# Top-k attention into a Sinkhorn mixture of experts, one core: low parts of the last group's weights and sums of stored outputs through accumulating DMAs, gates copied in a later turn

## The chip, the cores and the metric

The kernel runs on one core of a Trainium2 chip. A core has TensorE (PE in the profile; its weight loads are shown apart as PEld), VectorE (DVE), ScalarE (ACT), GpSimd (POOL) and SyncE (SP), each with a queue of its own that it works through in order, and 16 DMA engines that all queues share. SP issues nearly all DMAs of this kernel. The metric is the time of one execution on the device in microseconds, lower is better.

## The reference

```python
# attention: 4 batches, 8 heads, 576 positions, 64 wide
scores = (1/8) * q @ k.T
scores = where(scores >= the 32nd largest of the row, scores, -1e9)
attn   = softmax(scores);  out = attn @ v
x = out as [N=2304, D=512]
# mixture of experts, 8 experts, hidden width F=1024
P = exp(x @ w_gate - max)
8 times: P /= row sums + 1e-9;  P /= column sums + 1e-9;  P *= N / E
out = sum over e of P[:, e:e+1] * (relu(x @ w1[e]) @ w2[e])
```

The row and column scaling of P (Sinkhorn) is done on all 2304 rows at once, so no gate is known before the last row of attention is.

## The kernel before

The products are done in fp32r with every operand split into a high part (the value rounded to fp32r) and a low part (value minus high part); each product of the reference is three matmuls: high x high, high x low, low x high. A split is one ScalarE copy (`hi_act`, L83) and one subtraction, on GpSimd (`lo_pool`, L86) or VectorE (`lo_dve`, L89).

**Turns.** The 2304 rows are 18 pieces of 128 rows, 9 blocks of 256. Five blocks (`BOARD`) go through the experts in turns: a turn takes one expert for the blocks that are on board, two at a time in most turns. In a turn the expert's weights are loaded by SP (`wr`), split (`wh` on ScalarE, `wl` on GpSimd), the hidden layer is made (L469), stored as `hh` and `hl`, and the second layer is made (L584). The outputs of a turn aren't gated yet: ScalarE copies them to a tile `y` (L592) and SP stores them in DRAM (`spill`). `y` is a ring of four buffers (`YB`) that several steps share, among them `gates`. Turns 16 to 19 have two blocks on board, turns 20 to 23 one.

**Attention** runs beside the turns, at a higher priority: scores on TensorE (L122, L123), top-k on VectorE (L138, L141), exponentials on ScalarE, a transposition by DMA, and the weighing of the values on TensorE (L269). Its last stage belongs to turn 12. It ends with the gate logits (L387) and `sinkhorn`, whose eight rounds have one small matmul each (L444). Then `stages_until` calls `gates`, which transposes the gates of the last four blocks on TensorE (L715, into tile `pc`), copies them to two `y` tiles (L718) and stores them in DRAM, and `right_factors`, which makes the last group's right operands.

**Stored outputs.** `stored` takes the ungated outputs back, piece by piece: SP loads one to a `y` tile (L606), ScalarE multiplies it by its gate (L607), VectorE adds it to `acc` (L609); after eight experts SP writes the piece to the output. There are 80 such steps. `some` does two of them after a hidden tile of turns 20 to 23 (`feeding`), and two for each hidden call of the last group.

**The last group.** The other four blocks (`LAST`, 1024 rows) are done at the end, expert by expert, with Strassen's scheme in the Winograd form: seven products in place of eight. There are 64 calls, 32 of `hidden_pair` and 32 of `outputs_pair`. Each begins with `left_factors`: SP loads 512 KB of weights to a tile `wr` (named `wf` in rows, L682), GpSimd makes four sums `st` of its quarters (L690; also named `wf`), and both are split: `rh` and `rl` from `wr`, `sh` and `sl` from `st`. `wr` and `st` take turns in a ring of three buffers; `rh`, `rl`, `sh` and `sl` have two buffers each. Then come 42 matmuls (L708). `hidden_pair` gates its results (L747), and `all_factors` makes the right operands of the next products: differences on VectorE (L774), splits by L83 and L89.

The order in which instructions stand on each engine is made when the program is built, by a scheduler that goes by priorities and a model of the timeline; `tc.issue_after` ties an instruction behind another.

Of the kernel before, what the change touches and what calls it, by code (L numbers as in the profile page):

```python
# [44 lines left out]

PARKED = 4
ALONE, LATER = range(0, 4), range(4, 8)
WR, WB, XR, NS, RAW, YB, HF = 3, 6, 3, 3, 3, 4, 5


@with_exitstack
def kernel(
# [366 lines left out]
    def sinkhorn():  # L419
# [17 lines left out]
        for i in range(8):  # L437
# [8 lines left out]
            nc.vector.reciprocal(cr, cp)  # L446
            nc.vector.tensor_tensor(P if i == 7 else Q, Q, cr[:, None, :].to_broadcast([128, NT, E]), op=OP.mult)

    def convert(src, shape):
        wr = wp.tile(shape, F32, name="wr", bufs=WR)  # L450
        nc.sync.dma_start(wr, src)
        return split_weights(wr, shape)

    def split_weights(wr, shape):
# [6 lines left out]
    def products(ps, f0, seat, n, wh, wl, k0):  # L461
        nk = wh.shape[1]
        cs = slice(seat.c0, seat.c0 + n)
        for fo in range(512 // n):
            fs = slice((f0 + fo) * 128, (f0 + fo + 1) * 128)
            i = 0
            for kk in range(nk):
                for a, x in ((wh, seat.xh), (wh, seat.xl), (wl, seat.xh)):
                    nc.tensor.matmul(ps[:, fo, :], a[:, kk, fs], x[:, k0 + kk, cs],  # L469
                                     start=(i == 0), stop=(i == 3 * nk - 1))  # L470
                    i += 1

    def hidden(seat, n, s, wh, wl):
        m = 512 // n
        for f0 in range(0, 2, m):
            ps = ps1.tile([128, m, n], F32, name="p1")
            products(ps, f0, seat, n, wh, wl, 0)
            with tc.high_priority(offset=2 * BIG):
                done = store_hidden(seat, slice(2 * s + f0, 2 * s + f0 + m), slice(seat.c0, seat.c0 + n), ps)
            if feeding:  # L480
                some(done, 2)

# [53 lines left out]
            store_hidden(seat, ft, slice(0, 256), ps)  # L536

    def store_hidden(seat, ft, cs, src):
        nc.scalar.activation(seat.hh[:, ft, cs], src, AF.Relu)  # L539
        return nc.vector.scalar_tensor_tensor(seat.hl[:, ft, cs], src, 0.0, seat.hh[:, ft, cs].bitcast(F32),  # L540
                                              op0=OP.max, op1=OP.subtract)

    ready = {}

# [51 lines left out]
    def stored():  # L596
        for blk in BOARD:
            for piece in BLOCKS[blk]:
                t = tile_id[piece]
                acc = accp.tile([128, 512], F32, name="acc", bufs=2)  # L600
                for e in range(E):
                    g = P[:, t, e:e + 1]
                    y = acc if e == 0 else op_.tile([128, 512], F32, name="y", bufs=YB)
                    while (t, e) not in spill:
                        yield False
                    nc.sync.dma_start(y, spill[t, e])  # L606
                    nc.scalar.activation(y, y, AF.Copy, scale=g)  # L607
                    if e:
                        nc.vector.tensor_tensor(acc, acc, y, op=OP.add)  # L609
                    if e == E - 1:  # L610
                        store_rows(nc.sync, acc, piece)
                    yield True

    more = stored()

    def some(ins, n):
        with tc.issue_after(ins.ins):
            for _ in range(n):
                if not next(more, False):
                    break  # L620
# [55 lines left out]
        return f  # L676

    def left_factors(*src):
        wr = wf.tile([128, KD, 256], F32, name="wf", bufs=3)
        rows = KD // len(src)  # L680
        for i, w in enumerate(src):
            nc.sync.dma_start(wr[:, i * rows:(i + 1) * rows], w)  # L682
        a11, a21 = wr[:, 0:2, 0:128], wr[:, 0:2, 128:256]
        a12, a22 = wr[:, 2:4, 0:128], wr[:, 2:4, 128:256]
        st = wf.tile([128, 4, 2, 128], F32, name="wf", bufs=3)
        for i, (a, b, op) in enumerate((
            (a21, a22, OP.add), (st[:, 0], a11, OP.subtract),
            (a11, a21, OP.subtract), (a12, st[:, 1], OP.subtract),
        )):
            nc.gpsimd.tensor_tensor(st[:, i], a, b, op=op)  # L690
        raw = [wq.tile([128, 6, 128], F32R, name=f"r{p}", bufs=2) for p in "hl"]
        for r, a in ((slice(0, 4), wr[:, :, 0:128]), (slice(4, 6), a22)):
            hi_act(raw[0][:, r], a)
            lo_pool(raw[1][:, r], a, raw[0][:, r])
        sums = [ws.tile([128, 4, 2, 128], F32R, name=f"s{p}", bufs=2) for p in "hl"]
        hi_act(sums[0], st)
        lo_pool(sums[1], st, sums[0])
        f = {f"S{i + 1}": tuple(w[:, i] for w in sums) for i in range(4)}
        for i, name in enumerate(("A11", "A12", "A22")):
            f[name] = tuple(w[:, 2 * i:2 * i + 2] for w in raw)  # L700
        return f

    def product(ps, a, b, fresh):
# [8 lines left out]
    def gates():  # L712
        pt = [psx.tile([128, 512], F32, name="pc", bufs=2) for _ in range(2)]
        for i, piece in enumerate(p for blk in LAST for p in BLOCKS[blk]):
            nc.tensor.transpose(pt[i // 4][0:E, i % 4 * 128:i % 4 * 128 + 128], P[:, tile_id[piece], :], idt)  # L715
        for n in range(2):
            y = op_.tile([128, 512], F32, name="y", bufs=YB)
            nc.scalar.activation(y[0:E], pt[n][0:E], AF.Copy)  # L718
            nc.sync.dma_start(turned_gates[:, n, :], y[0:E])

    turned_gates = dram.tile([E, 2, 512], F32, name="gates")

    def spread_gates(e):
        G = []
# [7 lines left out]
    def hidden_pair(e, s, B, G):  # L732
# [33 lines left out]
        plus(c, c, u2)  # L766
        put(0, 1, c)
        product(u, A["A22"], B["T4"], False)
        some(put(1, 0, u), 2)
        return H  # L770

    def minus(a, b):
# [15 lines left out]
    def all_factors(top, b21, b22):  # L788
        f, t1, b12 = top
        t2 = minus(b22, t1)  # L790
        f["T1"] = halves_of(t1, lo_dve)
        t4 = minus(b21, t2)
        f["T2"] = halves_of(t2, lo_dve)
        f["B21"] = halves_of(b21, lo_dve)
        t3 = minus(b22, b12)
        f["T3"] = halves_of(t3, lo_dve)
        f["B22"] = halves_of(b22, lo_dve)
        f["T4"] = halves_of(t4, lo_dve)
        return f
# [59 lines left out]
    def stages_until(v):  # L859
# [7 lines left out]
        if not todo and not factors and free(NB * 2, v):  # L867
            with tc.high_priority(offset=BIG):
# [1 line left out]
                x2 = ctx.enter_context(tc.tile_pool(name="x2", bufs=1, side="right"))  # L870
                accp = ctx.enter_context(tc.tile_pool(name="accp", bufs=2, side="right"))
                unpark()
                gates()
                with tc.tile_pool(name="tm", bufs=3, side="right") as tm:
                    factors.update(right_factors(tm))
                wq = ctx.enter_context(tc.tile_pool(name="wq", bufs=2, side="right"))
# [11 lines left out]
    first.close()  # L888
    wf = ctx.enter_context(tc.tile_pool(name="wf", bufs=3))
    ws = ctx.enter_context(tc.tile_pool(name="ws", bufs=2))  # L890
    gp = ctx.enter_context(tc.tile_pool(name="gp", bufs=2))
# [77 lines left out]
```

## Time and profile before

| | |
|---|---|
| median of 3 runs (lowest to highest) | 2090.15 us (2083.6 to 2090.2) |
| the profiled execution | 2086.1 us, span 2084.3 us |
| busy over the span: PE, DVE, ACT, POOL | 1834 us, 1536 us, 1315 us, 1367 us |
[...]
| the last group | from 1305 us to the end |

Busy time is the sum of an engine's instructions; two matmuls that overlap count as one stretch. "Waits" are idle times of an engine with the instruction on another engine that ended them. [...]

### The profile page before, as it was taken

What the parts mean: (1) busy time and instruction counts of PE and PEld (TensorE: products, weight loads), DVE (VectorE), ACT (ScalarE), POOL (GpSimd) and SP (SyncE); (2) the same over time, 40 slices, a digit from 0 to 9 for tenths busy, and PEclk for the clock granted to TensorE, in tenths of its full rate; (3) what the DMA queues carried; (4) which work ended last, traced back from release to release, by engine and by line L of the source; (5) the groups of instructions that cost most, each with busy time, mean ns of one, the idle gap of its engine ahead of it and who ended that gap; (6) DMA issues with size and microseconds to landing.
All of it is one profiled execution on the core that took longest, in us unless ns stands there. A gap on an engine that the chain in (4) does not pass through costs nothing.

```text
span 2084.3 us, 26893 instructions
## 1 busy us (share of the span) xinstructions
PE 1834.3 (88%) x9137; PEld 1480.5 (71%) x9137; DVE 1536.0 (74%) x2443; ACT 1314.5 (63%) x1971; POOL 1367.0 (66%) x1079
## 2 busy tenths in 40 slices
PE   5899989999999999994279997988889888889887
PEld 3777778788787888783168887666667667667675
DVE  8999889797888678788321155678777877887775
ACT  5888889898998879987423355544434444344333
POOL 3478556555555665643444476889788788888883
PEclk9999999999999999996579998999999999999999
DMA  4787766756666656563123367322213122121111
GB/s 127 259 274 240 196 184 184 204 146 171 169 158 150 186 163 172 161 165 72 40 82 111 124 238 249 102 76 69 79 61 96 61 86 72 61 85 41 51 51 51
DMA packets 244746, 274.39 MB, mean 132 GB/s; under 512 B 144112, under 2 KB 166768, under 8 KB 244608
## 3 DMA queue, kind: packets, MB, share of 16 engines
q1 hardware_dynamic: 244608, 272.67, 43.9%
q8 instruction: 72, 1.18, 0.2%
q14 instruction: 66, 0.54, 0.1%
HBM read 205.73 MB, written 34.64 MB: 115 GB/s over the span
## 4 chain that ended last, share of the span: by engine, by line
PE 44%; POOL 17%; DVE 16%; ACT 8%; issue 8%; DMA 6%; SPq 0%; ACTq 0%; POOLq 0%; DVEq 0%
PE p L469 14%; PE p L584 14%; PE p L708 6%; POOL wf L690 6%; POOL sl L86 4%; DVE m L138 4%; POOL rl L86 4%; DVE w L141 3%; PE pc L708 3%; PE pt L269 3%; DVE hr L89 2%; DVE acc L609 2%; DMA wr<-in_w_dram 2%; DVE hf L774 2%; DMA turned<-halves 1%
## 5 line engine op out<-in xcount | busy, mean ns | idle before, releaser
L86 POOL TENSOR_TENSOR wl<-wr,wh 128x1024 fp32r<-128x1024 f32 x184 | 444.0, 2425 | 250.6 <-ACT wh L83 243.8
L138 DVE MAX8 m<-w 128x8 f32<-128x576 f32 x432 | 320.9, 753 | 6.0
L469 PE MATMUL p<-xh,wh 128*128 128x256 f32 (+1 forms) x800 | 273.7, 342 | 4.9 <-DVE hl L540 4.9
L469 PE MATMUL p<-xl,wh 128*128 128x256 f32 (+1 forms) x800 | 271.7, 340 | 1.8 <-DVE xl L89 1.8
L469 PE MATMUL p<-xh,wl 128*128 128x256 f32 (+1 forms) x800 | 271.9, 340 | 0.0
L690 POOL TENSOR_TENSOR wf<-wf 128x256 f32<-128x256 f32 x256 | 263.0, 1044 | 9.1 <-DMA wf<-in_w_dram 3.9
L584 PE MATMUL p<-wh,hh 128*128 128x512 f32 x640 | 250.8, 398 | 14.1 <-ACT hh L539 12.8
L540 DVE SCALAR_TENSOR_TENSOR hl<-p,hh 128x512 fp32r<-128x512 f32 x160 | 108.9, 683 | 194.5 <-ACT hh L539 167.0
L584 PE MATMUL p<-wl,hh 128*128 128x512 f32 x640 | 250.6, 393 | 0.0
L83 ACT ACTIVATE wh<-wr 128x1024 fp32r<-128x1024 f32 x184 | 193.5, 1058 | 90.2 <-DMA wr<-in_w_dram 60.1
L584 PE MATMUL p<-wh,hl 128*128 128x512 f32 x640 | 241.5, 393 | 0.0
L86 POOL TENSOR_TENSOR sl<-wf,sh 128x1024 fp32r<-128x1024 f32 x64 | 174.2, 2723 | 82.3 <-ACT sh L83 77.9
L141 DVE MATCH_REPLACE8 w<-m,w 128x576 f32<-128x576 f32 x288 | 213.8, 743 | 0.0
L89 DVE TENSOR_TENSOR hr<-hf,hq 128x1024 fp32r<-128x1024 f32 x96 | 178.6, 1871 | 6.0 <-ACT hq L83 6.0
L86 POOL TENSOR_TENSOR rl<-wf,rh 128x512 fp32r<-128x512 f32 (+1 forms) x128 | 165.4, 1307 | 23.4 <-ACT rh L83 23.4
L469 PEld LDWEIGHTS p<-xh,wh 128*128 128x128 f32 x800 | 156.0, 195 | 25.3 <-DVE hl L540 6.6
L138 DVE MAX8 m<-s 128x8 f32<-128x576 f32 x144 | 108.3, 752 | 86.5 <-ACT s L128 86.0
L469 PEld LDWEIGHTS p<-xl,wh 128*128 128x128 f32 x800 | 156.0, 195 | 17.8 <-DVE xl L89 2.2
L469 PEld LDWEIGHTS p<-xh,wl 128*128 128x128 f32 x800 | 155.8, 195 | 15.9 <-issue 0.9
L83 ACT ACTIVATE hq<-hf 128x1024 fp32r<-128x1024 f32 x112 | 114.5, 1051 | 82.8 <-DVE hf L774 50.9
L584 PEld LDWEIGHTS p<-wh,hh 128*128 128x128 f32 x640 | 121.2, 190 | 40.4 <-ACT hh L539 14.5
L83 ACT ACTIVATE sh<-wf 128x1024 fp32r<-128x1024 f32 x64 | 67.6, 1056 | 114.3 <-POOL wf L690 101.9
(197 smaller groups left out, 4650.1 us busy)
## 6 DMA issues: line engine op xcount, KB each, us to landing
wr<-in_w_dram SPq DMA_DIRECT2D x176, 512.0 KB, 3.9
y<-y SPq DMA_DIRECT2D x150, 256.0 KB, 3.5
wf<-in_w_dram SPq DMA_DIRECT2D x32, 512.0 KB, 3.5
wf<-in_w_dram SPq DMA_DIRECT2D x64, 256.0 KB, 3.2
raw<-in_k_dram SPq DMA_DIRECT2D x56, 288.0 KB, 3.7
raw<-in_q_dram SPq DMA_DIRECT2D x32, 256.0 KB, 3.4
p<-y SPq DMA_DIRECT2D x32, 256.0 KB, 4.4
wr<-in_w_dram SPq DMA_DIRECT2D x32, 256.0 KB, 4.7
```

Of the source, the lines that this page charges most:

```text
L83: nc.scalar.activation(dst, src, AF.Copy)
L86: nc.gpsimd.tensor_tensor(dst, src, hi.bitcast(F32), op=OP.subtract)
L89: nc.vector.tensor_tensor(dst, src, hi.bitcast(F32), op=OP.subtract)
L138: nc.vector.max(m8[:, u, r, :], ws[u] if r else units[u][0])
L141: nc.vector.match_replace(ws[u], m8[:, u, r, :], ws[u] if r else units[u][0], LOWEST)
L269: weighed = nc.tensor.matmul(av[r, 0:n], vr[:, o:o + 64], at[:, block, 0:n], start=(j == order[0]), stop=(j == order[-1]))
L469: nc.tensor.matmul(ps[:, fo, :], a[:, kk, fs], x[:, k0 + kk, cs], start=(i == 0), stop=(i == 3 * nk - 1))
L540: return nc.vector.scalar_tensor_tensor(seat.hl[:, ft, cs], src, 0.0, seat.hh[:, ft, cs].bitcast(F32), op0=OP.max, op1=OP.subtract)
L584: nc.tensor.matmul(ps, a[:, ft, ts], m[:, ft % 2, :], start=(i == 0), stop=(i == 3 * NFT - 1))
L609: nc.vector.tensor_tensor(acc, acc, y, op=OP.add)
L690: nc.gpsimd.tensor_tensor(st[:, i], a, b, op=op)
L708: nc.tensor.matmul(ps, w[:, kk, :], x[:, kk, :], start=(fresh and i == 0), stop=(i == 5), skip_group_check=True)
```

## The change

It has two parts.

In the last group, `left_factors` no longer subtracts on GpSimd. ScalarE writes the negated high part to the low tile (a copy with scale -1), and a DMA issued by GpSimd adds the source to it in place (`accum_op=OP.add`). The weights are loaded as four DMAs of 128 KB in place of one of 512 KB or two of 256 KB, so that A11, A12 and A22 lie side by side and the split of `wr` is one operation of 128x768. Stored outputs that are taken back in the last group are added to `acc` by such a DMA too, in place of VectorE; those in turns are multiplied and added in one VectorE operation, without ScalarE. The low part of B21 (16 of 112 splits) moves from VectorE to GpSimd.

`gates` is no longer called with the right factors but behind the first hidden tile of turn 21, and stored outputs are taken back from turn 21 on in place of turn 20, tied behind the turn's latest weight load as well.

```diff
     def hidden(seat, n, s, wh, wl):
...
             if feeding:
-                some(done, 2)
+                if not spread:
+                    with behind(matmul, done[0], fetched[-1]):
+                        gates()
+                some(FEED, done[1], fetched[-1])
...
                     nc.sync.dma_start(y, spill[t, e])
-                    nc.scalar.activation(y, y, AF.Copy, scale=g)
-                    if e:
-                        nc.vector.tensor_tensor(acc, acc, y, op=OP.add)
+                    if e == 0:
+                        nc.vector.tensor_scalar(acc, acc, g, None, op0=OP.mult)
+                    elif visiting:
+                        nc.vector.scalar_tensor_tensor(acc, y, g, acc, op0=OP.mult, op1=OP.add)
+                    else:
+                        nc.scalar.activation(y, y, AF.Copy, scale=g)
+                        nc.gpsimd.dma_start(acc, y, accum_op=OP.add)
...
     more = stored()
-
-    def some(ins, n):
-        with tc.issue_after(ins.ins):
+    visiting = True
+
+    @contextmanager
+    def behind(*which):
+        with ExitStack() as anchors:
+            for ins in which:
+                anchors.enter_context(tc.issue_after(ins.ins))
+            yield
+
+    def some(n, *which):
+        with behind(*which):
             for _ in range(n):
                 if not next(more, False):
                     break
...
     def left_factors(*src):
-        wr = wf.tile([128, KD, 256], F32, name="wf", bufs=3)
-        rows = KD // len(src)
+        wr = wf.tile([128, 4, 2, 128], F32, name="wf", bufs=3)
+        rows = 4 // len(src)
         for i, w in enumerate(src):
-            nc.sync.dma_start(wr[:, i * rows:(i + 1) * rows], w)
-        a11, a21 = wr[:, 0:2, 0:128], wr[:, 0:2, 128:256]
-        a12, a22 = wr[:, 2:4, 0:128], wr[:, 2:4, 128:256]
+            for k in range(0, rows, 2):
+                kh = (i * rows + k) // 2
+                for half, blk in ((0, kh), (1, 3 - kh)):
+                    nc.sync.dma_start(wr[:, blk], w[:, k:k + 2, half * 128:half * 128 + 128])
+        a11, a12, a22, a21 = (wr[:, i] for i in range(4))
...
-        raw = [wq.tile([128, 6, 128], F32R, name=f"r{p}", bufs=2) for p in "hl"]
-        for r, a in ((slice(0, 4), wr[:, :, 0:128]), (slice(4, 6), a22)):
-            hi_act(raw[0][:, r], a)
-            lo_pool(raw[1][:, r], a, raw[0][:, r])
-        sums = [ws.tile([128, 4, 2, 128], F32R, name=f"s{p}", bufs=2) for p in "hl"]
-        hi_act(sums[0], st)
-        lo_pool(sums[1], st, sums[0])
-        f = {f"S{i + 1}": tuple(w[:, i] for w in sums) for i in range(4)}
+        parts = []
+        for pool, name, src, m in ((wq, "r", wr[:, 0:3], 3), (ws, "s", st, 4)):
+            h, l = (pool.tile([128, m, 2, 128], F32R, name=name + p, bufs=2) for p in "hl")
+            hi_act(h, src)
+            nc.scalar.activation(l, src, AF.Copy, scale=-1.0)
+            nc.gpsimd.dma_start(l, src, accum_op=OP.add)
+            parts.append((h, l))
...
         product(u, A["A22"], B["T4"], False)
-        some(put(1, 0, u), 2)
+        put(1, 0, u)
+        some(2)
...
-        f["B21"] = halves_of(b21, lo_dve)
+        f["B21"] = halves_of(b21, lo_pool)
...
                 unpark()
-                gates()
...
-        feeding = turn > max(BOARD.values()) + 3
+        feeding = turn > max(BOARD.values()) + 4
```

The change moves instructions at two places that matter below.

TensorE at the end of attention, before: the weighing of the values (`at`), the logits, Sinkhorn's eight small matmuls (`cs`) and the transpositions of the gates (`P`) stand in one piece, and the next second-layer matmul of turn 16 (`p_10504`) stands behind them.

```order
L269 MATMUL pt<-at,values 64x256 x10
L269 MATMUL pt<-at,values 64x320 x10
L387 MATMUL pt<-wgs,xt 64x8 x32
L387 MATMUL pt<-wgs,xm 64x8 x8
L425 MATMUL pt<-idt,mx 128x128
L444 MATMUL pt<-cs,ones 128x8 x8
L715 MATMUL pc<-idt,P 8x128 x8
L584 MATMUL p_10504<-wh,hh 128x512
L584 MATMUL p_10504<-wl,hh 128x512
```

After, around the first of Sinkhorn's small matmuls (hidden-layer matmuls of two tiles `p` of turn 19, now line 471, on both sides of it):

```order
L471 MATMUL p_11135<-xh,wh 128x512
L471 MATMUL p_11135<-xl,wh 128x512
L471 MATMUL p_11135<-xh,wl 128x512
L444 MATMUL pt<-cs,ones 128x8
L471 MATMUL p_11156<-xh,wh 128x512
L471 MATMUL p_11156<-xl,wh 128x512
```

The eight small matmuls now stand one by one, 24 to 37 rows of turn work apart, and the transpositions of the gates stand between two hidden tiles of the single-block turns:

```order
L471 MATMUL p_11618<-xh,wh 128x256
L471 MATMUL p_11618<-xl,wh 128x256
L471 MATMUL p_11618<-xh,wl 128x256
L735 MATMUL pc<-idt,P 8x128 x8
L471 MATMUL p_11673<-xh,wh 128x256
```

GpSimd in the last group, before (`wf` on the left is `st`, on the right `wr`; one call's tiles have neighbouring numbers):

```order
L690 TENSOR_TENSOR wf_13766<-wf_13763 128x256 x2
L690 TENSOR_TENSOR wf_13766<-wf_13766,wf_13763 128x256
L690 TENSOR_TENSOR wf_13766<-wf_13763,wf_13766 128x256
L86 TENSOR_TENSOR sl_13778<-wf_13766,sh_13777 128x1024
L690 TENSOR_TENSOR wf_13834<-wf_13831 128x256 x2
L690 TENSOR_TENSOR wf_13834<-wf_13834,wf_13831 128x256
L86 TENSOR_TENSOR rl_13772<-wf_13763,rh_13771 128x512
L86 TENSOR_TENSOR rl_13772<-wf_13763,rh_13771 128x256
L690 TENSOR_TENSOR wf_13834<-wf_13831,wf_13834 128x256
L86 TENSOR_TENSOR sl_13846<-wf_13834,sh_13845 128x1024
```

After, at a like place:

```order
L710 TENSOR_TENSOR wf_14176<-wf_14171,wf_14176 128x256
L619 DMA acc_13736<-y_14087 128x512
L619 DMA acc_13736<-y_14091 128x512
L716 DMA sl_14187<-wf_14176 128x1024
L716 DMA rl_14182<-wf_14171 128x768
L710 TENSOR_TENSOR wf_14246<-wf_14241 128x256 x2
L710 TENSOR_TENSOR wf_14246<-wf_14246,wf_14241 128x256
L710 TENSOR_TENSOR wf_14246<-wf_14241,wf_14246 128x256
L86 TENSOR_TENSOR hr_14099<-hf_14027,hq_14097 128x1024
L716 DMA sl_14257<-wf_14246 128x1024
L716 DMA rl_14252<-wf_14241 128x768
```

The subtractions are gone and DMA issues stand in their place. In about three of four calls both DMAs of a call stand directly ahead of the next call's sums, `sl` first; in the others `rl` comes first.

## Rows read from the trace of the kernel before

**Rows 1.** The page's first part (busy, share, instructions) and clock by slices.
```profile
PE 1834.3 (88%) x9137; PEld 1480.5 (71%) x9137; DVE 1536.0 (74%) x2443; ACT 1314.5 (63%) x1971; POOL 1367.0 (66%) x1079
...
PEclk9999999999999999996579998999999999999999
```
**Rows 2.** Windows: length; busy of PE, PEld, DVE, ACT, POOL; granted clock, DMA share, GB/s.
```profile
956.00:1058.00 102.00, 33.26 (x198) 21.62 (x198) 59.47 (x155) 55.07 (x83) 36.66 (x45) 0.53 0.19 40
1058.00:1202.00 144.00, 144.00 (x645) 119.82 (x646) 17.10 (x25) 49.21 (x66) 59.84 (x26) 0.98 0.34 115
1202.00:1305.00 103.00, 88.19 (x517) 80.27 (x516) 58.61 (x43) 58.24 (x80) 70.78 (x29) 0.90 0.72 248
1305.00:2084.00 779.00, 676.77 (x2738) 527.42 (x2736) 593.88 (x612) 327.52 (x473) 635.55 (x464) 0.94 0.22 69
```
**Rows 3.** Timeline of PE, 939 to 1059 us: start, length, row, idle before and its releaser.
```profile
939.82 2.38 PE L269 MATMUL pt<-at,values 128*64 128x256 f32 x20
...
946.67 0.40 PE L469 MATMUL p<-xh,wl 128*128 128x512 f32 x1
...
993.21 4.53 PE L269 MATMUL pt<-at,values 128*64 128x256 f32 x20 [3.00 <-ACT at L165]
1018.41 4.87 PE L269 MATMUL pt<-at,values 128*64 128x320 f32 x20 [20.67 <-ACT at L188]
...
1032.30 0.56 PE L444 MATMUL pt<-cs,ones 128*128 128x8 f32 x2 [2.71 <-DVE cs L442]
1035.30 0.60 PE L444 MATMUL pt<-cs,ones 128*128 128x8 f32 x2 [2.43 <-DVE cs L442]
...
1057.99 0.79 PE L584 MATMUL p<-wh,hh 128*128 128x512 f32 x1 [1.15 <-ACT y L592]
```
**Rows 4.** Tile `y`, 940 to 1070 us: durations in ns, first and last start.
```profile
L592 ACT ACTIVATE y<-p x3: 569/570/597, 1057.4 to 1066.3; 128x512 f32<-128x512 f32 x3
...
L718 ACT ACTIVATE y<-pc x2: 569/578/586, 1056.1 to 1056.9; 8x512 f32<-8x512 f32 x2
```
**Rows 5.** Groups by form in the last group: GpSimd, VectorE, ScalarE (busy, mean ns | idle before).
```profile
L690 POOL TENSOR_TENSOR wf<-wf 128x256 f32<-128x256 f32 x256 | 263.0, 1044 | 9.1 <-DMA wf<-in_w_dram 3.9
L86 POOL TENSOR_TENSOR sl<-wf,sh 128x1024 fp32r<-128x1024 f32 x64 | 174.2, 2723 | 82.3 <-ACT sh L83 77.9 <-DMA wf<-in_w_dram 4.4
L86 POOL TENSOR_TENSOR rl<-wf,rh 128x512 fp32r<-128x512 f32 x64 | 97.9, 1530 | 23.4 <-ACT rh L83 23.4
L86 POOL TENSOR_TENSOR rl<-wf,rh 128x256 fp32r<-128x256 f32 x64 | 69.3, 1083 | 0.0
...
L89 DVE TENSOR_TENSOR hr<-hf,hq 128x1024 fp32r<-128x1024 f32 x96 | 178.6, 1871 | 6.0 <-ACT hq L83 6.0
L609 DVE TENSOR_TENSOR acc<-acc,y 128x512 f32<-128x512 f32 x42 | 55.1, 1311 | 0.0
...
L83 ACT ACTIVATE sh<-wf 128x1024 fp32r<-128x1024 f32 x64 | 67.6, 1056 | 114.3 <-POOL wf L690 101.9 <-PE p L708 12.2
```
**Rows 6.** Waits in the last group: who for whom, us in total, times, longest.
```profile
PE p L708 <- DVE hr L89: 24.4, 10, 2.7
PE p L708 <- POOL rl L86: 19.7, 16, 2.3
PE pc L708 <- POOL sl L86: 15.6, 15, 2.0
```
**Rows 7.** The chain, 1464 to 1468 us: twelve matmuls of the last group without a gap.
```profile
1464.42 2.72 PE p L708 x12
```
**Rows 8.** Lines 690 and 682: shortest, median and longest ns; issues of the weight loads, and landing.
```profile
L690 POOL TENSOR_TENSOR wf<-wf x256: 718/742/1777, 1304.6 to 2046.9; 128x256 f32<-128x256 f32 x128
L682 SPq DMA_DIRECT2D wf<-in_w_dram x96: 332/551/1589, 1299.6 to 2037.4; - x96
DMA to landing us min/median/max: 3.0/3.4/4.8
```
**Rows 9.** Line 606, the loads of stored outputs: issue to landing.
```profile
DMA to landing us min/median/max: 2.5/4.0/7.0
```

More of the change, by code (lines that the diff above doesn't have):

```diff
@@ L47 @@
 ALONE, LATER = range(0, 4), range(4, 8)
-WR, WB, XR, NS, RAW, YB, HF = 3, 6, 3, 3, 3, 4, 5
+WR, WB, XR, NS, RAW, YB, HF, FEED = 3, 6, 3, 3, 3, 4, 5, 2
 @with_exitstack
@@ L447, in sinkhorn @@
             nc.vector.tensor_tensor(P if i == 7 else Q, Q, cr[:, None, :].to_broadcast([128, NT, E]), op=OP.mult)
+    fetched = []
     def convert(src, shape):
         wr = wp.tile(shape, F32, name="wr", bufs=WR)
-        nc.sync.dma_start(wr, src)
+        fetched.append(nc.sync.dma_start(wr, src))
         return split_weights(wr, shape)
@@ L468, in products @@
                 for a, x in ((wh, seat.xh), (wh, seat.xl), (wl, seat.xh)):
-                    nc.tensor.matmul(ps[:, fo, :], a[:, kk, fs], x[:, k0 + kk, cs],
-                                     start=(i == 0), stop=(i == 3 * nk - 1))
+                    matmul = nc.tensor.matmul(ps[:, fo, :], a[:, kk, fs], x[:, k0 + kk, cs],
+                                              start=(i == 0), stop=(i == 3 * nk - 1))
                     i += 1
+        return matmul
     def hidden(seat, n, s, wh, wl):
@@ L476, in hidden @@
             ps = ps1.tile([128, m, n], F32, name="p1")
-            products(ps, f0, seat, n, wh, wl, 0)
+            matmul = products(ps, f0, seat, n, wh, wl, 0)
             with tc.high_priority(offset=2 * BIG):
@@ L538, in store_hidden @@
     def store_hidden(seat, ft, cs, src):
-        nc.scalar.activation(seat.hh[:, ft, cs], src, AF.Relu)
-        return nc.vector.scalar_tensor_tensor(seat.hl[:, ft, cs], src, 0.0, seat.hh[:, ft, cs].bitcast(F32),
-                                              op0=OP.max, op1=OP.subtract)
+        return (nc.scalar.activation(seat.hh[:, ft, cs], src, AF.Relu),
+                nc.vector.scalar_tensor_tensor(seat.hl[:, ft, cs], src, 0.0, seat.hh[:, ft, cs].bitcast(F32),
+                                               op0=OP.max, op1=OP.subtract))
     ready = {}
@@ L690, in left_factors @@
             nc.gpsimd.tensor_tensor(st[:, i], a, b, op=op)
-        raw = [wq.tile([128, 6, 128], F32R, name=f"r{p}", bufs=2) for p in "hl"]
-        for r, a in ((slice(0, 4), wr[:, :, 0:128]), (slice(4, 6), a22)):
-            hi_act(raw[0][:, r], a)
-            lo_pool(raw[1][:, r], a, raw[0][:, r])
-        sums = [ws.tile([128, 4, 2, 128], F32R, name=f"s{p}", bufs=2) for p in "hl"]
-        hi_act(sums[0], st)
-        lo_pool(sums[1], st, sums[0])
-        f = {f"S{i + 1}": tuple(w[:, i] for w in sums) for i in range(4)}
+        parts = []
[5 more added lines that the diff above has]
+            parts.append((h, l))
+        f = {f"S{i + 1}": tuple(w[:, i] for w in parts[1]) for i in range(4)}
         for i, name in enumerate(("A11", "A12", "A22")):
-            f[name] = tuple(w[:, 2 * i:2 * i + 2] for w in raw)
+            f[name] = tuple(w[:, i] for w in parts[0])
         return f
@@ L719, in gates @@
             nc.sync.dma_start(turned_gates[:, n, :], y[0:E])
+        spread.append(True)
     turned_gates = dram.tile([E, 2, 512], F32, name="gates")
+    spread = []
     def spread_gates(e):
@@ L885 @@
         stages_until(turn)
-        feeding = turn > max(BOARD.values()) + 3
+        feeding = turn > max(BOARD.values()) + 4
         visit(turn, [blk for blk in BOARD if BOARD[blk] <= turn < BOARD[blk] + E])
     first.close()
+    visiting = False
     wf = ctx.enter_context(tc.tile_pool(name="wf", bufs=3))
```

## The prediction

> **What bounds the kernel now.** The page's busy line comes first: no engine is full over the span, PE with 88% the nearest, and the clock row shows one dip, to 0.5 and 0.6 of full speed, in slices 19 and 20 [rows 1]. So the span has stages with different limits, and the windows by stage say which. From 956 to 1058 us PE is busy for 33 of 102 us at a clock of 0.53. From 1058 to 1202 it is full. From 1202 to 1305 it is busy for 88 of 103 us. In the last group it is busy for 677 of 779 us and POOL for 636 [rows 2].
>
> The dip: the timeline shows turn work on PE up to 947.1 us and then again from 1058.0. Between them stand only attention, Sinkhorn's eight small matmuls (one every 3.0 us, PE idle for 2.4 of them) and the gates [rows 3]. What the turn's matmul waited for is named in its row: ScalarE's copy of an output to `y`, L592. That copy could not start before 1057.4 because the two copies of the gates, which come ahead of it in the ring of four `y` buffers, ran only at 1056.1 and 1056.9 [rows 4]. The gates need Sinkhorn, Sinkhorn needs all of attention. So a ring of buffers ties turn 16's outputs to the end of Sinkhorn, and 111 us pass without turn work.
>
> The last group: 64 calls in 779 us are 12.17 us a call. PE's floor is 42 matmuls of 2.72 / 12 = 0.227 us, 9.5 us a call [rows 7]. GpSimd carries 636 / 64 = 9.9 us a call and waits 1.3 us for `sh` and 0.4 us for `rh` [rows 2, 5]; that makes 11.6 of the 12.17, so GpSimd's queue sets the pace. PE's idle time is 779 - 677 = 102 us, of which 35 us end on `rl` or `sl` and 24 us on VectorE's splits [rows 2, 6].
>
> **Part one: the gates move.** With the gates behind turn 21, the ring no longer ties turn 16. The order shows turn matmuls between all of attention's last ones, about 350 of them ahead of the last weighing of values. At 0.227 us [rows 7] that is 79 us, and with attention's own matmuls some 90, where attention took 71 us from 947 to 1018 alone [rows 3]. Another 360 (82 us) stand between there and the gates, where Sinkhorn took 1023 to 1055. So PE should seldom find attention late. What can be won is 111 us less the matmuls that still have to be done in there: 33 us at about half clock, and the same 20 matmuls take 2.38 us at 939.8 and 4.53 us at 993.2 [rows 3], so 17 us and a little for 947 to 956, 20 us. This leaves 91. Against it: VectorE, which was nearly the only one at work on top-k there (59 of 102 us, [rows 2]), and ScalarE (55 us) now share with turn work, and a late operand stops PE's queue. Upper end 91; lower end 60, if PE keeps a third of the waits. I take 80, near the upper end, because the order leaves attention 20 us of room and in the eighteen slices ahead of the dip, turns beside attention, PE kept its clock at 9 tenths or more [rows 1].
>
> Stored outputs in turns 20 to 23 fall from 32 to 24, and lose their ScalarE step. PE idles 15 us there [rows 2], and weight loads at 248 GB/s and a DMA share of 0.72 are the neighbour. Nothing is booked; the most would be a few microseconds.
>
> **Part two: the last group.** Off GpSimd go `sl` (2.72 us a call) and both `rl` (1.53 + 1.08), 341 us in all; onto it come two DMA issues a call and 49 of `acc`. VectorE loses the 42 additions (55 us) and 16 of 96 splits at 1.87 (30 us) [rows 5]. ScalarE gets 64 x (1.06 + about 0.8), 119 us, on top of 328 of 779 [rows 2, 5]: it stays below the others. If issues were free, GpSimd would have 300 us of work and PE would set the pace.
>
> But the transfer now stands in a loop. The ring of three `wf` buffers lets `st` of the next call be written only when this call's `wr` is read, so when DMA `rl` has landed. In three of four calls GpSimd's queue runs: four sums, DMA `sl` (which waits for both ScalarE copies of `st`), DMA `rl`, wait for its landing, four sums again. Before, the subtraction read `wr` in 2.6 us with nothing to wait for. The loop per call:
> - four sums at 0.9 us: 3.6. The median is 0.74 and the mean 1.04 [rows 5, 8]; I go between because less VectorE work with two operands collides with them.
> - two ScalarE copies at 1.06 [rows 5] with two handovers of 0.1: 2.3.
> - the issue of `sl`: no DMA issued by GpSimd is in this trace. Lower bound SP's shortest issue, 0.33 us [rows 8]; upper bound the subtraction itself, 2.72 [rows 5]. I take 1.0, nearer SP's, since nothing is computed.
> - issue to landing of `rl`, 384 KB: lower bound the shortest landing of a weight load, 3.0; upper bound the longest landing of a stored output, 7.0 [rows 8, 9]. I take 4.5, above the loads' median of 3.4, because an addition has to read two sides.
> - the DMAs on `acc` add an issue and, in pairs, a wait for the one before; calls with `rl` first save part: 0.2 on balance.
>
> Sum 11.6 us; the bounds give 8.6 and 16.2. Since 11.6 is above PE's 9.5, it counts: 64 x (11.6 - 12.17) = -37 us. The low end is not 8.6, because PE's floor and its waits that are not for `rl` and `sl`, (102 - 35) / 64 = 1.0, hold it at 10.5: -107 us.
>
> [...]
>
> The quartered weight loads (4 x 128 KB) are booked at nothing: a call's load is issued when the `sl` of two calls before it has landed, so about a call ahead of its use, and loads land in 3.0 to 4.8 us [rows 8]. Only when landing takes some 7 us longer does it enter the loop. B21's low part adds 16 x about 2.7 (as `sl`) = 43 us to GpSimd, in the shadow of the landing of `rl`; without that cover it costs 0.7 us a call.
>
> **Sum**, against the profiled execution's own 2086.1 us (4 us below the median of the runs shown, inside their spread): 2086 - 80 - 37 = 1969 us.
>
> **Rivals.**
> (a) Transfers land about as fast as loads (3 to 3.5 us, issue under 0.7): the loop falls to 9 to 10 us, PE sets the pace at 10.5. 2086 - 80 - 107 = 1899. For it: the landings of 3.4 us; against it: the addition's second read. [...]
> (b) Landing of 5.4 to 6 us: a loop of 12.5 to 13.1, so 20 to 60 us lost in the last group. 2026 to 2066, middle 2045. For it: 0.9 MB of transfers with additions in each call beside loads; landings of 4.0 at the median and 7.0 at the longest in a busy stretch [rows 9].
> (c) Slower: the same landing, at 7.0 us, makes the loop 14.1 and the last group 64 x 1.9 = 123 us longer; 2086 - 80 + 123 = 2129. It decides from a loop of 13.5, so from a landing of 6.4 us on. Against it: DMA engines are busy for 22% in this stage [rows 2].
> (d) The hole isn't filled, only moved: attention, sharing VectorE and ScalarE, ends later, and PE stops at each of its matmuls in the queue. Then part one gives 25 in place of 80: 2024. Against it: the room counted above.
>
> **How the numbers follow.** Forecast 45%, (a) 22%, (b) 18%, (c) 8%, (d) 7%. The likeliest alone lies between 1945 and 2000 (hole 70 to 91, loop 11.2 to 12.1). The range must leave out no more than 2 in 10: it takes in (a) from 1890 on, the forecast, (d) and most of (b), up to 2050. A measurement of this kernel tells 0.3%, about 6 us, from no change; (c), with a sliver of (b), makes slower 0.08, same 0.02, faster 0.90.
>
> **What would show it.** The dip of clock and PE between 947 and 1058 us is gone, and the last group begins near 1225 us. In the last group a call takes 11.6 us; GpSimd's busy time falls to about 300 us plus issues, but its sums wait for DMAs, and PE's waits for `rl` and `sl`, now on DMAs, stay. The forecast is wrong if a DMA issue on GpSimd takes over 2 us, if `rl` lands in less than 3.5 or more than 5.5 us, or if PE waits over 30 us for attention.

## The result, and the profile after

The changed kernel takes 2027.59 us (median of 4 runs, 2017.98 to 2030.56) against 2088.63 us of before beside it: a ratio of 0.9704, 95% interval 0.9666 to 0.9742. It is faster by 61 us where 117 were forecast. Its profiled execution took 2030.56 us, span 2028.7.

The page of the changed kernel, busy time and clock row:

```profile
PE 1819.7 (90%) x9137; PEld 1455.5 (72%) x9137; DVE 1417.0 (70%) x2388; ACT 1390.5 (69%) x2004; POOL 1167.8 (58%) x1080
...
PEclk9999999999999999999999999999999999999998
```

The dip of the clock row [rows 1] is gone, and GpSimd has 199 us less work. The windows of the same stages, in the columns of [rows 2], say where the time came from and where it went:

```profile
956.00:1058.00 102.00, 102.00 (x556) 81.80 (x556) 59.03 (x113) 81.32 (x120) 59.47 (x51) 1.00 0.52 139
1058.00:1121.00 63.00, 63.00 (x332) 54.27 (x331) 23.93 (x77) 26.61 (x34) 47.36 (x26) 1.00 0.39 128
1121.00:1209.00 88.00, 78.81 (x467) 70.23 (x466) 45.09 (x38) 36.05 (x45) 61.68 (x25) 0.94 0.73 248
1209.00:2028.00 819.00, 681.28 (x2739) 514.87 (x2737) 483.13 (x560) 425.70 (x539) 438.17 (x465) 0.97 0.70 156
```

From 956 us to the last group PE has 1355 matmuls (1360 before) and needs 253 us in place of 349. Of the 96 us, 74 are idle time (9 in place of 84, before rounding 9.2 and 83.6) and 22 are busy time (244 us in place of 265): the matmuls of the first stage ran at a granted clock of 1.00, full speed, where it had been 0.53. The gates' eight transposing matmuls now stand at 1133.5 us, and nothing waits for them. Then the last group gives 40 back: 819 in place of 779. PE's busy time there is 681 as against 677; its idle time went from 102 to 138.

GpSimd's queue in the last group, by groups of instructions with their issues of DMAs (busy, mean ns | idle before, releasers), where [rows 5] had the subtractions:

```profile
L710 POOL TENSOR_TENSOR wf<-wf 128x256 f32<-128x256 f32 x256 | 217.7, 866 | 157.7 <-DMA sl<-wf 110.0 <-DMA rl<-wf 21.6 <-DMA wf<-in_w_dram 19.8
L86 POOL TENSOR_TENSOR hr<-hf,hq 128x1024 fp32r<-128x1024 f32 x32 | 83.3, 2604 | 5.3 <-ACT hq L83 5.2
L716 POOL DMA_DIRECT2D rl<-wf x64 | 61.1, 955 | 39.9 <-ACT rl L715 39.1 <-DMA wf<-in_w_dram 0.8
L716 POOL DMA_DIRECT2D sl<-wf x64 | 58.4, 912 | 94.6 <-issue 42.1 <-ACT sl L715 24.7 <-ACT y L764 22.3
L619 POOL DMA_DIRECT2D acc<-y x49 | 43.8, 893 | 58.5 <-DMA acc<-y 20.6 <-ACT y L618 15.9 <-PE p L728 11.2
```

In these rows 464 us are work (438 where records that overlap count once) and 356 are standing. 158 us are sums that wait, 132 of them for landings of `sl` and `rl`. 193 are issues that wait: 102 of them for ScalarE (64 for its copies to `rl` and `sl`, 38 for copies to `y`), 42 with no releaser in the profile. So GpSimd got lighter and still sets a pace, now by what it waits for. PE waits on the other side of the same transfers, where [rows 6] had 15.6 and 19.7 us:

```profile
PE pc L728 <- DMA sl<-wf: 61.1, 45, 5.4
PE p L728 <- DMA rl<-wf: 31.4, 27, 3.0
```

Line 716 issues `rl` and `sl`. Its row of landings, and the DMA queues of the last group (packets, MB, share of 16 engines; q0 are GpSimd's):

```profile
DMA to landing us min/median/max: 3.8/5.4/8.9
```
```profile
q0 software_dynamic: 25488, 71.58, 47.0%
q1 hardware_dynamic: 82259, 55.77, 22.8%
```

Which landing ends the sums' wait? One call in GpSimd's timeline (start, length):

```profile
1469.99 0.89 POOL L716 DMA_DIRECT2D sl<-wf  x1 [0.30 <-POOL hr L86]
1470.58 1.20 POOL L716 DMA_DIRECT2D rl<-wf  x1
1474.54 2.94 POOL L710 TENSOR_TENSOR wf<-wf 128x256 f32<-128x256 f32 x4 [2.77 <-DMA sl<-wf]
```

This `rl` landed 5.8 us after its issue, at 1476.3, when the next call's sums had been running for 1.8 us. So the sums waited for `sl`, not for `rl`. There are 63 steps from one call to the next. In 54 of them the first sum starts within 0.15 us of the landing of the call's transfer that was issued first (43 times `sl`, 11 times `rl`); in 45 `rl` lands only after that start. `wr` and `st` thus don't simply take turns in the ring: the next `st` seems to get whichever buffer comes free first, though the trace doesn't name buffers. From first sum to first sum a call takes 12.4 us, where it took 11.7 before: 4.2 for the sums with what stands between them, 2.6 from there to the first issue, 5.3 from this issue to its landing, 0.3 to the next sum (means).

### The profile page after: what moved, and what is told of

Its sections match the earlier page's. It is cut to its first block, busy times and chain, and to the rows that moved or that the text cites. A ratio compares the mean times of both kernels' runs of the same rounds, so it can differ in the third digit from the quotient of the medians.

```text
span 2028.7 us, 27366 instructions
## 1 busy us (share of the span) xinstructions
PE 1819.7 (90%) x9137; PEld 1455.5 (72%) x9137; DVE 1417.0 (70%) x2388; ACT 1390.5 (69%) x2004; POOL 1167.8 (58%) x1080
## 3 DMA queue, kind: packets, MB, share of 16 engines
q0 software_dynamic: 25488, 71.58, 19.0%
## 5 line engine op out<-in xcount | busy, mean ns | idle before, releaser
L710 POOL TENSOR_TENSOR wf<-wf 128x256 f32<-128x256 f32 x256 | 217.7, 866 | 157.7 <-DMA sl<-wf 110.0
L83 ACT ACTIVATE wh<-wr 128x1024 fp32r<-128x1024 f32 x184 | 193.5, 1059 | 84.9 <-DMA wr<-in_w_dram 67.7
L841 DVE TENSOR_TENSOR acc<-p,acc 128x512 f32<-128x512 f32 x124 | 85.2, 688 | 105.1 <-PE p L728 104.9
L89 DVE TENSOR_TENSOR hr<-hf,hq 128x1024 fp32r<-128x1024 f32 x80 | 120.7, 1517 | 46.5 <-ACT hq L83 46.5
L590 PEld LDWEIGHTS p<-wh,hh 128*128 128x128 f32 x640 | 121.0, 190 | 36.9 <-ACT hh L545 12.7
L590 PEld LDWEIGHTS p<-wl,hh 128*128 128x128 f32 x640 | 121.2, 190 | 24.4 <-POOL wl L86 0.7
```

The costliest lines, as they stand in the source:

```text
L83: nc.scalar.activation(dst, src, AF.Copy)
L89: nc.vector.tensor_tensor(dst, src, hi.bitcast(F32), op=OP.subtract)
L590: nc.tensor.matmul(ps, a[:, ft, ts], m[:, ft % 2, :], start=(i == 0), stop=(i == 3 * NFT - 1))
L841: nc.vector.tensor_tensor(ACC[dd, i, n], ps, ACC[dd, i, n], op=OP.add)
```

## The experiments

The theories: **A**, GpSimd's queue runs in a loop through the ring of three `wf` buffers, and a landing stands in it. **B**, TensorE waits for the landings itself, because `rl` and `sl` have two buffers. **C**, the 16 DMA engines carry too much traffic, and all transfers land late. **D**, added after eight runs, the stored outputs' transfers into `acc` cost the group twice, by contention and by their place in GpSimd's queue. Ratios are to the kernel before.

PE in the last group, from the windows (from 1209 us to the end; before from 1305, the group alone from 1304): length, busy, the difference, granted clock.

| kernel | time, us | group | PE busy | PE idle | clock |
|---|---|---|---|---|---|
| before | 2089 | 779 | 677 | 102 | 0.94 |
| changed | 2027.6 | 819 | 681 | 138 | 0.97 |
| gates alone | 1991.3 | 782 | 676 | 106 | 0.93 |
| group alone | 2135.2 | 833 | 696 | 137 | 0.94 |
| `sl`, `acc` on DMAs | 1964.1 | 758 | 666 | 92 | 0.95 |
| `rl`, `acc` on DMAs | 1990.0 | 784 | 677 | 107 | 0.94 |
| `rl`, `sl` on DMAs | 2047.3 | 837 | 702 | 135 | 0.93 |
| `sl` alone on DMAs | 1964.3 | 753 | 659 | 94 | 0.95 |
| no accumulating DMAs, new layout | 1988.4 | 782 | 683 | 99 | 0.92 |
| `sl` alone, B21 on VectorE | 1974.2 | 766 | 668 | 98 | 0.95 |

**1. The gates' part alone.** The last group's `left_factors`, additions and B21 are those of before; the turns are the changed kernel's. Against the changed kernel:

```diff
+        raw = [wq.tile([128, 6, 128], F32R, name=f"r{p}", bufs=2) for p in "hl"]
...
-                        nc.gpsimd.dma_start(acc, y, accum_op=OP.add)
+                        nc.vector.tensor_tensor(acc, acc, y, op=OP.add)
```

> Part one alone: the gates and the stored outputs stand where the change puts them, the last group is that of before. If the two parts add, the start of the last group stays near 1209 us as in the changed kernel and the group takes its old 780 us: 1993 us in all, faster than both kernels. Rival: the last group of before profits from what stands ahead of it (loads, finished stored outputs) and gives part of the gain back: 2010 to 2030 us.

1991.26 us (1988.4 to 1993.36), ratio 0.9537 (0.9514 to 0.956). The first sum of the last group stands at 1204.9 us. The part is worth 98 us.

**2. The last group's part alone.** The reverse: `gates` and the turns as before. Against the kernel before:

```diff
+            nc.scalar.activation(l, src, AF.Copy, scale=-1.0)
+            nc.gpsimd.dma_start(l, src, accum_op=OP.add)
...
+                        nc.gpsimd.dma_start(acc, y, accum_op=OP.add)
```

> Part two alone: the gates stand ahead of turn 16's outputs again, the last group has the accumulating DMAs, the quartered loads and B21 on GpSimd. If the parts add: 2089 + 40 = 2129 us, slower than before, with PE idle from 947 to 1058 us. Rival: the last group is only slower because the shorter way to it leaves more stored outputs to it; then about 2090 us.

2135.22 us (2133.81 to 2139.54), ratio 1.0225 (1.0197 to 1.0252): 46 us slower. The two parts make -52 together where the whole change makes -61: they add up to within 9 us. `sl` lands in 5.0 and `rl` in 5.4 us at the median: the long landing needs nothing of the turns' part.

**3 and 4. One accumulating transfer in place of two.** Either `rl` or `sl` goes back to GpSimd; the stored outputs stay on DMAs. Run 3, against the changed kernel; run 4 has `"r"` in the condition:

```diff
-            nc.scalar.activation(l, src, AF.Copy, scale=-1.0)
-            nc.gpsimd.dma_start(l, src, accum_op=OP.add)
+            if name == "s":
+                nc.scalar.activation(l, src, AF.Copy, scale=-1.0)
+                nc.gpsimd.dma_start(l, src, accum_op=OP.add)
+            else:
+                lo_pool(l, src, h)
```

> The changed kernel, but rl is subtracted on GpSimd again (one operation of 128x768); sl and acc stay on accumulating DMAs. Theory A, the loop through the ring of three (the next call's sums wait for the landing of rl): the loop is 3.5 us of sums, 2.3 of ScalarE copies, 0.9 of issue, 2 of subtraction and 2 of the rest, so 11 us a call, 1920 to 1940 us. Theory B, TensorE waits for the landings themselves because rl and sl have two buffers each: only the waits for rl go, 1985 to 2005 us. Theory C, DMA engines shared by too much traffic: 0.5 MB in place of 0.9 MB a call, landings of sl near 4.4 us, 1985 to 2005 us.

> The changed kernel, but sl is subtracted on GpSimd again; rl and acc stay on accumulating DMAs. Theory A: the landing of rl still stands in the loop, with sl's 2.5 us of subtraction in place of an issue: 12.3 us a call, 1995 to 2010 us, and so slower than with sl alone on a DMA. Theory B: the waits of TensorE for sl, the larger ones, go: 1950 to 1970 us, faster than with sl alone on a DMA. Theory C: the landing of rl falls to near 4.2 us, 1980 to 2000 us, both variants alike.

With `sl` on a DMA 1964.1 us (1962.5 to 1969.58), ratio 0.9412 (0.9387 to 0.9437); with `rl` 1990.02 us (1986.16 to 1995.44), ratio 0.9533 (0.9506 to 0.9561). B had expected the other order and falls. A had this order, but 1920 to 1940 us for run 3 and 1995 to 2010 for run 4; C had both alike. No theory had run 3's time. GpSimd's queue in run 3, in the columns from above:

```profile
L710 POOL TENSOR_TENSOR wf<-wf 128x256 f32<-128x256 f32 x253 | 226.2, 913 | 25.6 <-DMA sl<-wf 13.6 <-DMA wf<-in_w_dram 6.7
L86 POOL TENSOR_TENSOR rl<-wf,rh 128x768 fp32r<-128x768 f32 x64 | 134.7, 2105 | 52.4 <-ACT rh L83 52.1
L86 POOL TENSOR_TENSOR hr<-hf,hq 128x1024 fp32r<-128x1024 f32 x32 | 93.6, 2926 | 0.5 <-ACT hq L83 0.5
L717 POOL DMA_DIRECT2D sl<-wf x64 | 59.8, 934 | 86.7 <-ACT y L767 38.7 <-ACT sl L716 27.5 <-PE p L731 10.3
```

The sums wait 26 us in place of 158. GpSimd computes 135 us more and the group takes 61 us less. In run 4 they wait for weight loads, which SP issues (L703) when `rl` has landed; the second row counts SP's standing, most of which costs nothing:

```profile
L710 POOL TENSOR_TENSOR wf<-wf 128x256 f32<-128x256 f32 x252 | 246.5, 1017 | 66.6 <-DMA wf<-in_w_dram 58.2 <-DMA rl<-wf 4.9
SPq L703 <- DMA rl<-wf: 464.8, 59, 14.7
```

With one subtraction on GpSimd, a buffer comes free in GpSimd's own queue, ahead of the next sums. Of 63 steps, 9 (run 3) and 3 (run 4) have a first sum that waits for a landing of `sl` or `rl` and starts within 0.15 us of it, in place of 54. The landings, of `sl` in run 3 and of `rl` in run 4:

```profile
DMA to landing us min/median/max: 4.4/4.4/9.4
```
```profile
DMA to landing us min/median/max: 3.8/3.8/5.9
```

In both the median is the shortest: 4.4 us for 512 KB, 3.8 for 384 KB. The third size is `acc`, 256 KB, whose shortest landing in the changed kernel was 3.2. These three fit 2.0 us and 0.6 for each 128 KB, which is 218 GB/s (131,072 bytes in 0.6 us), an estimate from the three.

Why 5.4 in the changed kernel? GpSimd's timeline there shows two `rl` with what stands beside them (start, length):

```profile
1521.18 0.86 POOL L716 DMA_DIRECT2D rl<-wf  x1
1523.06 0.86 POOL L716 DMA_DIRECT2D sl<-wf  x1 [1.01 <-DMA wf<-in_w_dram]
...
1555.88 0.86 POOL L619 DMA_DIRECT2D acc<-y  x1 [3.17 <-DMA acc<-y]
1556.42 1.21 POOL L716 DMA_DIRECT2D sl<-wf  x1
1558.06 0.86 POOL L716 DMA_DIRECT2D rl<-wf  x1 [0.43 <-ACT rl L715]
```

The first, issued ahead of its `sl`, landed in 3.8 us; the second, 1.64 us behind its `sl` (and 2.18 behind an `acc`), in 6.7. The same tile's row for each of them alone:

```profile
DMA to landing us min/median/max: 3.8/3.8/3.8
```
```profile
DMA to landing us min/median/max: 6.7/6.7/6.7
```

It is so for the whole group. Take the `rl` beside little plain traffic (under 200 KB moved by q1 in the 3.8 us behind the issue). The 10 with no accumulating transfer in flight at their issue landed in 3.8 us at the median and 3.9 at the longest; the 39 with one in flight took 5.7 at the median.

Beside plain traffic these transfers land later as well. Run 10 below has `sl` as its only accumulating transfer, one a call, and still its row of landings is:

```profile
DMA to landing us min/median/max: 4.4/4.5/9.3
```

What the queues moved in the 4.4 us behind the issue of the `sl` that landed in 9.3 us (packets, MB, share of 16 engines), and below it the same for one that landed in 4.4:

```profile
q1 hardware_dynamic: 914, 0.96, 65.5%
q0 software_dynamic: 20, 0.08, 9.3%
```
```profile
q0 software_dynamic: 144, 0.52, 60.2%
q1 hardware_dynamic: 139, 0.24, 14.6%
```

Of run 10's 64, the 35 with under 200 KB of plain traffic in that time landed in 4.4 us at the median; the 21 with 400 KB or more took 6.0. (One without any plain traffic beside it still took 6.0; why isn't shown.) So C falls as a theory of runs 3 and 4, which it had alike, but its ground, late landings beside plain traffic (6.0 us against 4.4 for run 10's `sl`), was measured just as those behind another accumulating transfer were (5.7 us against 3.8 for `rl`). By what mechanism either comes about isn't shown.

**5 to 7. Deeper rings.** A fourth `wf` buffer, or a third for `sl`, needs 4 KB of each partition. They were taken from `y` (two buffers in place of four), with a control (run 5, the first line of the diff alone). Run 6 has the second change too, run 7 `bufs=3` for `sl` in its place.

```diff
-WR, WB, XR, NS, RAW, YB, HF, FEED = 3, 6, 3, 3, 3, 4, 5, 2
+WR, WB, XR, NS, RAW, YB, HF, FEED = 3, 6, 3, 3, 3, 2, 5, 2
...
-        wr = wf.tile([128, 4, 2, 128], F32, name="wf", bufs=3)
+        wr = wf.tile([128, 4, 2, 128], F32, name="wf", bufs=4)
```

> The changed kernel with two `y` buffers in place of four, which frees 4 KB of each partition for the next two kernels; a control. All theories: the stored outputs and the outputs of the group have half the room, so 2025 to 2055 us, and the last group's sums on GpSimd still wait for the landings for 130 to 170 us.

> Two `y` buffers and four `wf` buffers: `wr` and `st` have two each, so that a call's sums no longer stand in a buffer that the call before it still reads. Theory A (the loop through the ring of three: sums, copies, issue, landing, next sums): the sums' waits for landings, 158 us, fall below 60, the last group from 820 to 745 to 775 us, the time to 1955 to 1985. Theory B (TensorE waits for a landing because `sl` and `rl` have two buffers) and theory C (the 16 DMA engines are shared by too much traffic): within 12 us of the control with two `y` buffers.

> Two `y` buffers and three buffers for `sl` in place of two, so that ScalarE's negated copy and GpSimd's issue need not wait for the matmuls that read `sl` two calls earlier. Theory B: TensorE's waits for `sl`, 142 us with its weight loads, fall below 70 and the time to 1960 to 1995. Theories A and C: within 12 us of the control with two `y` buffers.

The control 2114.63 us (ratio 1.0095 to 1.0134), the ring of four 2119.44 (1.0109 to 1.0163), the third `sl` 2129.29 (1.016 to 1.0212). The control alone is 87 us behind the changed kernel: the room of `y` is worth far more than was expected. GpSimd's sums in the control and, below, with four `wf` buffers:

```profile
L710 POOL TENSOR_TENSOR wf<-wf 128x256 f32<-128x256 f32 x256 | 235.1, 933 | 138.8 <-DMA sl<-wf 81.8 <-DMA wf<-in_w_dram 46.4 <-DMA rl<-wf 7.0
```
```profile
L710 POOL TENSOR_TENSOR wf<-wf 128x256 f32<-128x256 f32 x256 | 230.1, 926 | 166.6 <-DMA wf<-in_w_dram 148.1 <-DMA rl<-wf 11.6 <-DMA sl<-wf 1.1
```

The deeper ring did take the sums off the landings (89 us to 13), but they then waited for weight loads. SP, in order as well, stood at these loads until an earlier `sl` had landed, and at loads of stored outputs (L612) until a `y` buffer came free:

```profile
SPq L703 <- DMA sl<-wf: 267.6, 41, 15.0
SPq L612 <- DVE pc L773: 148.1, 26, 10.7
```

So the landing had only moved to the next queue: in 40 of 62 calls the first weight load was issued within 0.3 us of the landing of `sl` two calls before. A's forecast for this kernel missed by 135 us; B and C had the outcome, within 12 us of the control. A ring of four alone buys nothing when the next queue is tied as tightly. The third `sl`, B's kernel, is 15 us slower than the control, which no theory had. Neither ring was tried without taking from `y`.

**8. More plain traffic.** One more plain transfer of 512 KB a call.

```diff
+        for w in src:
+            idle = dram.tile(list(w.shape), F32, name=f"idle{len(src)}", bufs=4)
+            nc.sync.dma_start(idle, w)
```

> The changed kernel with one more plain transfer a call, the call's 512 KB of weights once more from DRAM to a DRAM tile that nothing reads, issued by SP behind the loads. It tells why `rl` and `sl` land in 5.4 us together and in 3.8 and 4.4 alone. If the 16 DMA engines are shared (theory C): the landings lengthen to 6 us or more, the last group by 20 to 60 us, the time is 2045 to 2090. If the two accumulating transfers only stand in each other's way in GpSimd's own queue: the landings stay between 5.2 and 5.6 us and the time within 12 us of the changed kernel's, 2016 to 2040.

2104.71 us (2094.9 to 2112.0), ratio 1.0068 (1.0046 to 1.009), and it answers another question than mine. Nothing tied the copies to the group, and the scheduler put all 96 at the program's start, from 17.0 to 136.7 us (first and last start in the row):

```profile
L706 SPq DMA_DIRECT2D idle<-in_w_dram x96: 488/510/1690, 17.0 to 136.7; - x96
```

The kernel is 77 us slower than the changed one, and its last group begins 73 us later (first sum at 1281.8 us in place of 1209.0). So the run doesn't test C. In the group, where they weren't, the landings stayed at 5.2 (`sl`) and 5.6 us (`rl`).

**9 to 12. The stored outputs, the layout, B21.** Run 9 is the changed kernel with the additions to `acc` on VectorE; run 10 that with only `sl` on a DMA; run 11 that with neither, so without any accumulating DMA; run 12 is run 10 with the low part of B21 on VectorE (the second piece of the diff).

```diff
-                        nc.gpsimd.dma_start(acc, y, accum_op=OP.add)
+                        nc.vector.tensor_tensor(acc, acc, y, op=OP.add)
...
-        f["B21"] = halves_of(b21, lo_pool)
+        f["B21"] = halves_of(b21, lo_dve)
```

> The changed kernel with the stored outputs of the last group added to `acc` on VectorE again, as before the change, and `rl` and `sl` by accumulating DMAs. Theory D: the 49 transfers into `acc` cost the group twice, since each lengthens the landings beside it and its issue stands in GpSimd's queue until ScalarE's `y` and the `acc` transfer before it are done (59 us of GpSimd's waits in the changed kernel's last group): the group loses 25 to 50 us, the time is 1977 to 2003. Theory A (the loop of sums, copies, issue and landing of `rl` and `sl` alone): within 12 us of the changed kernel, 2016 to 2040.

> Only `sl` by an accumulating DMA; `rl` on GpSimd and the stored outputs on VectorE. In the run with `sl` and `acc` on DMAs `sl` landed in 4.4 us where no other accumulating transfer was in flight and in 6.9 beside one of `acc`. Theory D: all land in 4.4 to 5 us and TensorE's waits for `sl`, 148 us there with its weight loads, fall below 110; 1935 to 1955. Theory A: 1957 to 1972, the time of that run.

> The changed kernel without a single accumulating DMA: all subtractions of `left_factors` on GpSimd, the stored outputs on VectorE; the 128 KB loads, the wider split, the low part of B21 on GpSimd and the gates' place stay. Beside the kernel with the gates' move alone (1991 us) it tells what the other layout is worth. If the landings and their queue are all that costs (theories A and D): within 15 us of 1991, since GpSimd's work a call is the same but one instruction less. If the layout itself costs or gains (loads in four pieces, B21): outside 1975 to 2006.

> Only `sl` by an accumulating DMA, and the low part of B21 back on VectorE. GpSimd has 16 subtractions of 2.4 us less, VectorE 16 of 1.2 us more. If GpSimd's queue still sets the loop (theory A): 8 to 25 us less than with B21 on GpSimd. If TensorE waits for landings and ScalarE instead: within 6 us of it.

Run 9: 2047.27 us (2040.4 to 2053.92), ratio 0.9792 (0.9768 to 0.9815), 20 us slower than the changed kernel, not 25 to 50 faster. D falls. GpSimd's queue in it:

```profile
L710 POOL TENSOR_TENSOR wf<-wf 128x256 f32<-128x256 f32 x256 | 215.9, 862 | 180.9 <-DMA sl<-wf 145.0 <-DMA wf<-in_w_dram 27.9 <-DMA rl<-wf 3.9
...
L716 POOL DMA_DIRECT2D sl<-wf x64 | 56.3, 879 | 155.1 <-ACT sl L715 64.2 <-ACT y L764 59.7 <-issue 22.0
L716 POOL DMA_DIRECT2D rl<-wf x64 | 56.0, 875 | 73.4 <-ACT rl L715 71.0 <-issue 2.3
```

The 102 us of the `acc` transfers left the queue and came back as waits: 229 us in place of 135 ahead of the other issues, 181 in place of 158 ahead of the sums. PE's idle time stayed (135 and 138 us); its matmuls took 21 us longer, at a granted clock of 0.93 against 0.97. What set the clock isn't shown.

Run 10: 1964.27 us (1953.16 to 1967.13), ratio 0.9393 (0.937 to 0.9416), the same as run 3, as A had it. Run 11: 1988.4 us (1987.07 to 1993.1), ratio 0.9519 (0.9503 to 0.9534), within 3 us of run 1: four loads of 128 KB, the split in one piece and B21 on GpSimd are together worth nothing. Run 12: 1974.22 us (1970.6 to 1979.13), ratio 0.9444 (0.9425 to 0.9463), 10 us slower than run 10. Both theories in its expectation are wrong on it: less work on GpSimd made its sums wait longer for `sl` (55 us, 27 in run 10).

The best versions are runs 3 and 10, 1964 us: the gates' move, and only `sl` by an accumulating DMA. They beat both kernels.

## Why the prediction was right and where it was wrong

- **Part one, -80, measured -96 to -98.** The mechanism was right: `y`'s ring tied turn 16 to Sinkhorn, and without the tie PE is busy without a gap from 939 to 1121 us. Two sizes were off, both on the cautious side. I kept 11 us for late operands of attention beside turn work; PE waited for none. And I counted the idle time in the hole only: another 6 us came from the stored-output stage, idle for 9 us in place of 15. Rival (d) is out.
- **Part two, -37, measured +40 (+46 alone): wrong in its sign.** Three steps failed: the base, the wait and the size of the loop.
- **The base.** 12.17 us a call is the whole group divided by 64. It holds the stretch behind the last sum, 2046.9 us to the end at 2084.3 [rows 8], which a shorter loop doesn't shorten. From first sum to first sum the loop took 11.7 us (1304.6 to 2042.8 us, 63 steps). Against that a loop of 11.6 gains about 7 us, not 37.
- **The wait.** The prediction lets the next call's sums wait "when DMA `rl` has landed". They waited for the transfer that was issued first, in 43 of 54 cases `sl`, and mostly began before `rl` landed.
- **The size.** The loop is 12.4 us, not 11.6; against 11.7 that is 41 us over the group, the whole loss. Sums with what stands between them took 4.2 (forecast 3.6), the stretch to the first issue 2.6 (2.3 for ScalarE's copies), the rest 0.3 (0.2). The collision with VectorE is in the traces: of the 256 sums of before, the 118 that ran beside its two-operand work of L89, L774 and L609 took 1.40 us at the mean, the other 138 at most 0.77; after, the 60 beside L89 and L797 took 1.20, the other 196 0.76. Of the two handovers of 0.1, the one from the last sum to ScalarE's copy took 0.03 us, the one from its negated copy to the issue 0.30 in the changed kernel (medians of those that were waited for). From the first issue to its landing it was 5.3, where the issue of `sl` and the landing of `rl` had 1.0 + 4.5. That these agree is luck, since it is another transfer. `rl` itself had 5.5 at the median in place of 4.5, though alone it lands in 3.8. What I left out is the other transfers: `sl`, `rl` and `acc` all go through q0 (its 71.58 MB are theirs), and beside little plain traffic an `rl` with another of them in flight took 5.7. That an addition reads two sides was the reason given for more than 3.4; no run tests it.
- **The term for `acc`, 0.2, was too small on paper (1.6 us a call of issues and waits) and too large in effect:** with `acc` off the queue the group is no shorter.
- **Rival (b)** is what came in the last group by its numbers: landings of 5.3 and 5.5 us, 819 / 64 = 12.8 us a call, 40 us lost. With the 96 us of part one it gives the measured time. Its ground, "transfers with additions in each call beside loads", holds as far as it goes. The forecast of 1969 us missed by 59; that the time lies in the range is owed to the room made for (b) and to a part one 16 us better than forecast.
- **Why one transfer less helps:** a landing no longer stands between most calls. In the three kernels with both transfers and four `y` buffers (the changed one, runs 2 and 9), 51 to 54 of 63 steps have a sum that waits for a landing and starts right behind it, and the loop takes 12.4 to 12.7 us. With one transfer (runs 3, 4, 10 and 12) it is 3 to 27 steps, and with one or none the loop takes 11.4 to 11.8. PE's idle time in the group goes with it: 135 to 138 us in the three, 92 to 107 in runs 1, 3, 4, 10, 11 and 12. Not settled is how much of the 36 us between them is the lengthening of the landing and how much that it stands in the loop at all: run 9's landings were 0.4 us shorter at the median and it gained nothing, and a landing made shorter with the queue left alone wasn't tried. Also open is why PE is busy for 659 us in one kernel and 702 in another with the same matmuls; the granted clock, 0.92 to 0.97, goes only partly with it.

## What to carry to other kernels

When work moves from an engine to a DMA, price the whole queue that the DMA goes through: the lone landing (here 3.8 us for `rl`), plus what was issued just ahead of it in that queue (5.7 with another in flight) and the plain traffic beside it (for a lone `sl` 6.0 beside 400 KB or more, 4.4 beside little), plus the wait of the issuing engine for its operand (here 64 us for ScalarE's copies to `rl` and `sl`). Then find in the trace which landing frees the buffer that the next step needs. Against the same kernel with none (run 11), `sl` alone was worth 24 us (run 10), and `sl` and `rl` together cost 59 (run 9). With `acc` on DMAs as well, `rl` was worth nothing (run 4) and both cost 39 (the changed kernel). Compare a loop with the old loop, not with the stage divided by its calls. A ring of buffers that two unrelated steps share (here `y`, for the gates and for the turns' outputs) is worth following first: it was 98 us, and halving it cost 87.

## What the hardware showed that I had not expected

- The shortest landings of accumulating DMAs issued by GpSimd were 3.2, 3.8 and 4.4 us for 256, 384 and 512 KB, which fit 2.0 us and 218 GB/s, an estimate. An `rl` with another of them in flight ahead, beside little plain traffic, took 5.7 us at the median (3.8 without). A lone `sl` beside 400 KB or more of plain traffic took 6.0 at the median, and 9.3 at the longest (4.4 beside little).
- Their issue held GpSimd for 0.87 us (`rl`, `acc`) and 0.88 (`sl`) at the median in the changed kernel, though the sizes differ by a factor of two.
- Plain loads of 128 KB landed in 2.6 us at the median beside all of this in the changed kernel's last group, with the DMA engines 70% busy.
